# Loading part of w2's last row into five slots of 24 other partitions, in a one-core adaLN decode block

## The chip, the cores and the metric

The kernel runs on one core of one Trainium2 chip. The metric is device time in microseconds (us) of that core. Three runs of the kernel before gave 235.51, 235.61 and 235.60 us, median 235.6.

## What is computed

One decode step of a transformer block for a batch of two tokens, all in float32: a modulation by `c`, attention over the last 4096 places of a key/value cache, and a feed-forward part with SiLU.

```python
mod = (_silu(c) @ w_mod).reshape(c.shape[0], 6, 1, -1)
sa, ca, ga, sb, cb, gb = (mod[:, 0], mod[:, 1], mod[:, 2], mod[:, 3], mod[:, 4], mod[:, 5])
h = _layernorm(x, axis=-1) * (1 + ca) + sa
x = x + ga * _A_ref(h, A_k_cache, A_v_cache, A_wq, A_wo)   # 32 heads of 128, 8 of keys/values
h = _layernorm(x, axis=-1) * (1 + cb) + sb
x = x + gb * _B_ref(h, B_w1, B_w2)                         # silu(h @ w1) @ w2
return x
```

The batch is 2, the width D is 512 and the hidden width F is 1792. The weights and the used part of the cache come to 97.5 MB, each byte of which is read from memory once.

## The kernel before

**Order of the loads.** One engine's queue, SP, issues every large load, in program order: `w_mod`, `wq`, then eight pairs of cache pieces (4 MB each), `wo` in two loads, `w1` in two (L511 to L514: 2688 KB, then 896 KB), and `w2` in four (L599 to L604: 2048, 768, 512 and 256 KB). They land in a ring of eight slots of 16 KB in each of the 128 partitions, so a load waits until what stood in its slot has been used. The hardware counts landings in semaphores. The framework that builds the program gives each load from SP or ACT one of eight such semaphores (DMAHW0 to DMAHW7), in the order of the issues, and makes a load wait until the load that used the same semaphore before it, eight issues earlier, has landed.

**The feed-forward part.** Row `f` of `w2` with `f = 14 p + t` lies in partition `p` as tile `t` of 14, each of 512 columns. The hidden vector is `uT` (L659), laid out in the same way with 32 columns for each `t`, of which columns 0 and 16 hold the two tokens. TensorE takes `uT[:, t]` as weights and `w2`'s tile `t` as moving data:

- tiles 0 to 7 with 512 columns at a time into the bank `acc_yw`, each tile in one of four groups of 32 output partitions (L661 to L669)
- tiles 8 to 10 into `acc_y`, where each of the four groups takes 128 of the 512 columns (L671 to L679)
- `gather` (L548) copies `acc_yw` to SBUF, one half on ACT and the other on VectorE, and adds its four groups up into `acc_y` with four matmuls
- tiles 11 to 13 into two banks `acc_l` of 64 columns for each group (L684 to L694). Tile 13 is the last load

VectorE then multiplies by `gb`, adds the residual (L696 to L704), and SP stores 4 KB (L706). `busy` (L564) runs matmuls whose result is thrown away.

**What sets the order.** All of this is written with `inorder` (L312), which keeps the written order on its engine, so on TensorE everything from `acc_yw` on stands as the program has it. SP, TensorE and VectorE each do their own list in order, and a wait at the head of a list holds all that stands behind it.

Of the kernel before, what the change touches and what calls it, by code (L numbers as in the profile page):

```python
# [10 lines left out]
ALU = mybir.AluOpType  # L11
AX = mybir.AxisListType

P = 128
B, D = 2, 512
HQ, HKV, DH = 32, 8, 128
G = HQ // HKV
F = 1792
EPS = 1e-5
RING = 8  # L20


@with_exitstack
def adaln_block(
# [19 lines left out]
    nc = tc.nc  # L44
# [16 lines left out]
    def const(shape, name):  # L61
        return consts.tile(shape, F32, name=name)

    def bank(tag, name):
        return (psum1 if tag in "CO" else psum).tile([P, 512], F32, tag=tag, name=name)


    slots, turn_of = ring.tile([P, RING, 4096], F32, name="slots"), [0]

    def stream(n=1):  # L70
        i = turn_of[0]
        if n % 2 == 0:
# [15 lines left out]
    def load_runs(w, per, lo, hi):  # L88

        e = w.shape[1]  # L90
        n = -(-(hi - lo) * e // 4096)
        t = stream(n)[:, : (hi - lo) * e].rearrange("p (q e) -> p q e", e=e)
        nc.sync.dma_start(t, w.rearrange("(p q) e -> p q e", q=per)[:, lo:hi, :])
        return t
# [5 lines left out]
    ident = const([P, P], "ident")  # L100
# [6 lines left out]
    for b in range(B):  # L107
# [53 lines left out]
    odd = const([P, 2], "odd")  # L161
    nc.vector.tensor_reduce(
        odd, ident.rearrange("p (a r) -> p r a", r=2), axis=AX.X, op=ALU.add
    )

    selg0, selg = const([P, G], "selg0"), const([P, B, G], "selg")
# [42 lines left out]
    qbd = [const([P, 4, B, 4, 32], f"qbd{n}") for n in range(2)]  # L209
# [11 lines left out]
    def silu_exp(t, name, shape):  # L221

        e = once.tile(shape, F32, tag="silu", name=name)
        nc.vector.tensor_scalar(e, t, -1.0, 87.0, op0=ALU.mult, op1=ALU.min)
        nc.scalar.activation(e, e, AF.Exp)
        nc.vector.tensor_scalar(e, e, 1.0, None, op0=ALU.add)
        nc.vector.reciprocal(e, e)
        return e
# [64 lines left out]
    hT, uT = const([P, 4, 32], "hT_b"), const([P, F // P, 32], "uT")  # L293
# [6 lines left out]
    for n in range(2):  # L300
        for k in range(4):
            wv = wqt[:, k, :].rearrange("p (n s g m) -> p n g s m", n=2, s=4, g=G)
            for g in range(G):
# [4 lines left out]
                    start=(k == 0),  # L308
                    stop=(k == 3),
                )  # L310

    inorder = tc.keep_in_program_order  # L312
# [199 lines left out]
    for lo, hi in ((0, 3), (3, 4)):  # L512
        wt = load_runs(w1, 4, lo, hi)
        w1t.extend(wt[:, k, :] for k in range(hi - lo))  # L514

    rx = once.tile([P, B, HKV // 2, 2, G], F32, tag="rx", name="rx")
    for b in range(B):
        nc.vector.tensor_mul(
# [5 lines left out]
    for r in (0, 64):  # L524
# [4 lines left out]
            start=True,  # L529
            stop=True,  # L530
# [33 lines left out]
    def busy(n):  # L564

        for _ in range(n):
            inorder(nc.tensor.matmul(  # L567
                junk[0:32, :],
                id4,
                quad.rearrange("p m y -> p (m y)"),  # L570
                start=True,
                stop=True,
            ))
# [5 lines left out]
    for q in range(28):  # L579
        g = q % 4  # L580
# [4 lines left out]
            start=(q < 4),  # L585
            stop=(q >= 24),
        ))
    for q in range(28, 32):
        for g in range(4):
# [4 lines left out]
                start=(q == 28),  # L594
                stop=False,
            ))
    gather(ao, acc, "acc_o_sb", False, True)
    busy(1)
    T2, WIDE = F // P, 8  # L599
    w2t = {}  # L600
    for lo, hi in ((0, WIDE), (WIDE, 11), (11, 13), (13, T2)):
        wt = load_runs(w2, T2, lo, hi)
        for tt in range(lo, hi):
            w2t[tt] = wt[:, tt - lo, :]  # L604
    aoT = once.tile([P, 4, 32], F32, tag="zp", name="aoT")
    nc.vector.transpose(aoT, ao.rearrange("p (m k) -> p k m", k=4))
    x1T = once.tile([P, 4, B], F32, tag="x1T", name="x1T")
# [19 lines left out]
    for k in range(4):  # L627
        for g in range(4):
# [4 lines left out]
                start=(k == 0),  # L633
                stop=(k == 3),
# [22 lines left out]
        )  # L657
    sg = silu_exp(z, "sgh", [P, T2, B])
    nc.vector.tensor_mul(uT[:, :, 0:32:16], z, sg)  # L659
    yw = bank("D", "acc_yw")  # L660
    for tt in range(WIDE):  # L661
        g = tt % 4
        inorder(nc.tensor.matmul(  # L663
            yw[32 * g : 32 * g + 32, :],
            uT[:, tt, :],
            w2t[tt],
            start=(tt < 4),
            stop=(tt >= WIDE - 4),
        ))  # L669
    y = bank("D", "acc_y")[:, :P]  # L670
    for tt in range(WIDE, 11):  # L671
        for g in range(4):
# [4 lines left out]
                start=(tt == WIDE),  # L677
                stop=False,
# [2 lines left out]

    H = P // 2
    yl = [bank("A", f"acc_l{h}")[:, :H] for h in range(2)]
    for tt in range(11, T2):  # L684
        for h in range(2):
            for g in range(4):
                lo = g * P + h * H
                inorder(nc.tensor.matmul(
                    yl[h][32 * g : 32 * g + 32, :],
                    uT[:, tt, :],  # L690
                    w2t[tt][:, lo : lo + H],
                    start=(tt == 11),
                    stop=(tt == T2 - 1),
                ))  # L694
    yp = once.tile([P, P], F32, tag="xp", name="yp")
    inorder(nc.vector.tensor_mul(yp, y, gb))  # L696
    inorder(nc.vector.tensor_add(yp, yp, x1))
# [1 line left out]
    for h in range(2):  # L699
        r = slice(h * H, (h + 1) * H)  # L700
        inorder(nc.vector.tensor_mul(yo[:, r], yl[h], gb[:, r]))
    for h in range(2):
        r = slice(h * H, (h + 1) * H)
# [30 lines left out]
```

## Time and profile before

| what | us |
|---|---|
| time, median of three runs | 235.6 |
| profiled execution, first to last instruction (its span) | 233.7 |
| median of the runs less that span | 1.9 |
| TensorE busy | 160.2 |
| VectorE busy | 115.6 |
| ScalarE busy | 28.5 |
| chain that ended last: share that is a transfer | 60% |

Of the profiled execution only the span is recorded, no time of its own beside it. The span is the time of one execution under the profiler, so times in the trace are compared with each other, and the 1.9 us is what the runs add around it.

To read it: a transfer is moved by 16 DMA engines at once. A row of the timeline gives the start and the length of a group of instructions that follow each other on one engine; SPq is SP's own list, in which an entry's length is the time of the issue, not of the transfer. The list of DMA issues gives the time from an issue to the landing of the whole load, where something waited for it. TensorE does a float32 matmul in two passes, so it shows twice as many records as the program has matmuls.

### The profile page before, as it was taken

The page shows a single profiled execution, that of the slowest core. Times are in us where ns is not written, and L with a number is a line of the kernel's source. Part 1 is how long each engine was busy: PE and PEld are TensorE (multiplying, and loading weights), DVE is VectorE, ACT ScalarE, POOL GpSimd, SP SyncE. Part 2 cuts the span into 40 slices and gives each one's busy share as a digit, 9 for nine tenths or more (in the row PEclk, how much of TensorE's full clock was granted, in tenths as well). Part 3 has the DMA queues.
Part 4 walks back from the last instruction along what each step waited for, and adds up shares of the span by engine and source line. Part 5 has one row for each costly group of instructions (what it writes and reads, how often), then busy time and mean ns, then how long its engine had stood idle before and what let it go on. Part 6 is the DMA issues. An engine that isn't in the chain of part 4 may idle for free.

```text
span 233.7 us, 2571 instructions
## 1 busy us (share of the span) xinstructions
PE 160.2 (69%) x1070; PEld 43.1 (18%) x1070; DVE 115.6 (49%) x179; ACT 28.5 (12%) x64; POOL 10.6 (5%) x35
## 2 busy tenths in 40 slices
PE   0005916959577839787689759758769777869784
PEld 0001401211111111221111202201112122314223
DVE  3004140178795758696197189249559540101232
ACT  1100210000311120120210201111030031002020
POOL 8600010000000000000000000000000000000000
PEclk9999975879979997999979988999997999999999
DMA  7998998999999999999999999999999999989991
GB/s 269 446 520 381 426 471 359 440 443 428 415 421 449 440 443 421 421 423 449 443 437 426 415 429 449 437 437 429 404 444 443 437 423 471 446 362 427 423 412 57
DMA packets 3795, 97.68 MB, mean 418 GB/s; under 512 B 433, under 2 KB 457, under 8 KB 969
## 3 DMA queue, kind: packets, MB, share of 16 engines
q1 hardware_dynamic: 3768, 97.53, 97.2%
q8 instruction: 8, 0.13, 0.2%
q14 instruction: 3, 0.02, 0.0%
q10 hardware_dynamic: 16, 0.00, 0.0%
HBM read 97.53 MB, written 0.00 MB: 417 GB/s over the span
## 4 chain that ended last, share of the span: by engine, by line
DMA 60%; issue 17%; DVE 14%; PE 6%; POOL 1%; POOLq 0%; SPq 0%; ACT 0%; DVEq 0%
DMA slots<-in_A_k_cache_dram 22%; DMA slots<-in_A_wq_dram 14%; DMA slots<-in_B_w_dram 12%; DMA slots<-in_A_v_cache_dram 12%; DVE kT L363 11%; PE q L304 3%; PE o L450 2%; DVE zp L422 1%; PE acc_yw L663 1%; DVE xp L420 1%; PE acc_y L673 0%; DVE xc L102 0%; POOL qg L321 0%; DVE qT L317 0%; PE acc_y L554 0%
## 5 line engine op out<-in xcount | busy, mean ns | idle before, releaser
L363 DVE STREAM_TRANSPOSE kT<-slots 128x1024 f32<-128x1024 f32 x64 | 73.7, 1210 | 22.9 <-DMA slots<-in_A_k_cache_dram 22.8
L376 PE MATMUL s<-kT,qbd 128*32 128x512 f32 x256 | 68.5, 703 | 17.9 <-DVE kT L363 17.0
L450 PE MATMUL o<-slots,ptb 128*32 128x512 f32 x256 | 29.1, 595 | 2.2 <-DMA slots<-in_A_v_cache_dram 2.2
L376 PEld LDWEIGHTS s<-kT,qbd 128*32 128x32 f32 x256 | 9.8, 113 | 66.9 <-DVE kT L363 62.9
L271 PE MATMUL m_a<-slots,scT 128*32 128x256 f32 x32 | 4.4, 507 | 20.4 <-DVE scT L263 20.4
L304 PE MATMUL q<-slots,hq_T 128*32 128x512 f32 x64 | 9.7, 773 | 7.4 <-DMA slots<-in_A_wq_dram 7.4
L450 PEld LDWEIGHTS o<-slots,ptb 128*32 128x32 f32 x256 | 7.7, 109 | 16.7 <-issue 16.6
L406 ACT COPY bias<-bp 128x1 f32<-128x1 f32 x8 | 1.3, 159 | 75.8 <-PE bp L404 75.8
L386 DVE TENSOR_REDUCE mx<-s 128x1 f32<-128x512 f32 x8 | 5.5, 691 | 9.6 <-PE s L376 9.6
L567 PE MATMUL junk<-quad,id 128*32 128x512 f32 x22 | 10.2, 596 | 0.0
L437 ACT ACTIVATE ptb<-pT,odd 128x256 f32<-128x256 f32 x16 | 6.7, 472 | 26.0 <-PE pT L429 26.0
L422 DVE TENSOR_TENSOR zp<-xp,quarter 128x1024 f32<-128x1024 f32 x8 | 9.8, 1225 | 0.2
L429 PE MATMUL pT<-zp,mix 128*32 128x256 f32 x64 | 5.8, 438 | 4.0 <-DVE zp L422 4.0
L317 DVE STREAM_TRANSPOSE qT<-q 128x512 f32<-128x512 f32 x2 | 1.4, 717 | 13.5 <-PE q L304 12.0
L581 PE MATMUL acc_o<-slots,oTn 128*32 128x512 f32 x56 | 6.2, 593 | 2.3 <-DMA slots<-in_A_wo_dram 2.3
L460 ACT COPY ob<-o 128x512 f32<-128x512 f32 x8 | 4.7, 586 | 24.4 <-PE o L450 24.4
L552 DVE COPY acc_o_sb<-acc_o 128x256 f32<-128x256 f32 x1 | 0.4, 425 | 14.1 <-ACT acc_o_sb L551 14.1
L388 PE MATMUL mT<-ident,mx 128*1 128x128 f32 x16 | 3.0, 270 | 6.3 <-DVE mx L386 6.3
L420 DVE STREAM_TRANSPOSE xp<-pr 128x512 f32<-128x512 f32 x8 | 5.5, 685 | 3.4 <-ACT pr L408 3.4
L257 DVE STREAM_TRANSPOSE cT<-xc 128x128 f32<-128x128 f32 x1 | 0.4, 401 | 13.7 <-DMA xc<-in_c_dram 13.7
L274 PE MATMUL m_sp<-slots,scT 128*32 128x512 f32 x32 | 7.2, 730 | 0.0
L468 PE MATMUL o_all<-ob,selh 128*64 128x128 f32 x64 | 5.9, 313 | 0.8 <-ACT ob L460 0.8
(140 smaller groups left out, 93.7 us busy)
## 6 DMA issues: line engine op xcount, KB each, us to landing
slots<-in_A_k_cache_dram SPq DMA_DIRECT2D x8, 4096.0 KB, 27.6
slots<-in_A_v_cache_dram SPq DMA_DIRECT2D x8, 4096.0 KB, 27.7
slots<-in_w_mod_dram SPq DMA_DIRECT2D x1, 6144.0 KB, 17.2
slots<-in_A_wo_dram SPq DMA_DIRECT2D x1, 6144.0 KB
slots<-in_B_w_dram SPq DMA_DIRECT2D x1, 2688.0 KB
slots<-in_A_wo_dram SPq DMA_DIRECT2D x1, 2048.0 KB, 29.5
slots<-in_B_w_dram SPq DMA_DIRECT2D x1, 2048.0 KB
slots<-in_B_w_dram SPq DMA_DIRECT2D x1, 896.0 KB
```

The lines of the kernel that those rows point to most:

```text
L274: nc.tensor.matmul(m_sp[r, :], scT[:, k, :], cd[:, g], start=(k == 0), stop=(k == 3))
L304: nc.tensor.matmul(q_ps[n][32 * g : 32 * g + 32, :], hq_T[:, k, :], wv[:, n, g], start=(k == 0), stop=(k == 3),)
L363: inorder(nc.vector.transpose(kT[s, j][:, 32 * c : 32 * c + 32, :], kt[s].rearrange("p (n j r) -> p j n r", j=4, r=32)[:, j, 32 * c : 32 * ...
L376: inorder(nc.tensor.matmul(s_ps[s][r : r + 32, :], qbd[h // 4][:, h % 4, b, j, :], kT[s, j][:, 32 * c : 32 * c + 32, e:32:2], start=(j == ...
L420: inorder(nc.vector.transpose(xp, pr[s]))
L422: inorder(nc.vector.tensor_mul(zp, xp[:, None, :, 0:16].to_broadcast([P, 4, 16, 16]), quarter[:, :, None, None].to_broadcast([P, 4, 16, 16 ...
L429: inorder(nc.tensor.matmul(tp[32 * i : 32 * i + 32, :], mix.rearrange("p v e -> p (v e)"), zp.rearrange("p y t x -> p (y t) x")[:, :, 4 * ...
L437: inorder(nc.scalar.activation(ptb[s % 2][:, :, e, :], tp.rearrange("p (w z) -> p w z", z=16), AF.Copy, scale=odd[:, e : e + 1],))
L450: inorder(nc.tensor.matmul(o_ps[s][r : r + 32, :], ptb[s % 2][:, w].rearrange("p e z -> p (e z)"), vt[s].rearrange("p (c w m f d) -> p c f ...
L468: inorder(nc.tensor.matmul(o_all[r : r + 64, :], selh[:, m, lo : lo + 2 * HQ], o_sb[s][:, m * DH : (m + 1) * DH], start=(s == 0 and m < 2) ...
L567: inorder(nc.tensor.matmul(junk[0:32, :], id4, quad.rearrange("p m y -> p (m y)"), start=True, stop=True,))
L581: inorder(nc.tensor.matmul(acc[32 * g : 32 * g + 32, :], oTn[:, q, :], wot[q], start=(q < 4), stop=(q >= 24),))
```

## The change

In the last of the 14 tiles of `w2`, columns 384 to 511 (the last group of 128) of partitions 8 to 127 no longer come with the last load. Those 120 pieces of 512 bytes go to 24 other partitions (0 to 11 and 32 to 43), five to a partition, in eight loads of 3 by 5 pieces that stand in the program right behind `w1`'s second load. The place they go to is `qbd[0]`, which held queries for the first half of the heads and is free by then. The last load becomes two: 8 partitions of 128 columns, and 128 partitions of 384 columns.

So that the matmuls find the hidden values in the same partitions, a product with a 0/1 matrix `away` moves them: `uj` is `uT`'s last tile spread over five slots by `slot`, `up` is the product on TensorE, and VectorE copies it into `uF`. The last group's 128 columns are then made by five matmuls of 48 partitions and one of 8 in each half, in place of one of 128.

```diff
+NE, NR, NJ = 3, 4, 5
...
+    own = P - 2 * NR * NJ * NE
+    away, slot = const([P, 48], "away"), const([P, NJ], "slot")
+    nc.gpsimd.memset(away, 0.0)
+    for h in range(2):
+        nc.vector.tensor_reduce(
+            away[:, 32 * h : 32 * h + NE * NR].rearrange("p (e r) -> p e r", e=NE),
...
+        )
+    nc.vector.tensor_reduce(
+        slot,
...
+    )
...
+    T2, WIDE = F // P, 8
+    w2p = w2.rearrange("(p t) e -> p t e", t=T2)
+    spare = qbd[0].rearrange("p s b j c -> p (s b j c)")
+    far = spare[:, : NJ * P].rearrange("p (j m) -> p j m", j=NJ)
+    uF = spare[:, NJ * P : NJ * (P + 32)].rearrange("p (j n) -> p j n", j=NJ)
+    uj = spare[:, NJ * (P + 32) : NJ * (P + 32 + B)].rearrange("p (j b) -> p j b", j=NJ)
+    nc.gpsimd.memset(uF, 0.0)
+    for h in range(2):
+        for r in range(NR):
+            lo = own + 60 * h + NJ * NE * r
+            nc.sync.dma_start(
+                far[32 * h : 32 * h + NE * NR].rearrange("(e r) j m -> e r j m", r=NR)[:, r],
+                w2p[lo : lo + NJ * NE, T2 - 1, D - P :].rearrange("(j e) m -> e j m", e=NE),
+            )
...
-    T2, WIDE = F // P, 8
     w2t = {}
-    for lo, hi in ((0, WIDE), (WIDE, 11), (11, 13), (13, T2)):
+    for lo, hi in ((0, WIDE), (WIDE, 11), (11, 13)):
         wt = load_runs(w2, T2, lo, hi)
         for tt in range(lo, hi):
             w2t[tt] = wt[:, tt - lo, :]
+    w2l = stream(1)[:, :D]
+    nc.sync.dma_start(w2l[0:own, D - P :], w2p[0:own, T2 - 1, D - P :])
+    nc.sync.dma_start(w2l[:, : D - P], w2p[:, T2 - 1, : D - P])
...
     nc.vector.tensor_mul(uT[:, :, 0:32:16], z, sg)
+    nc.vector.tensor_mul(
+        uj,
+        uT[:, T2 - 1, 0:32:16][:, None, :].to_broadcast([P, NJ, B]),
+        slot[:, :, None].to_broadcast([P, NJ, B]),
+    )
...
+    up = bank("C", "up")[:48, : NJ * B]
+    inorder(nc.tensor.matmul(
+        up, away, uj.rearrange("p j b -> p (j b)"), start=True, stop=True
+    ))
+    nc.vector.tensor_copy(uF[:48, :, 0:32:16], up.rearrange("p (j b) -> p j b", b=B))
     y = bank("D", "acc_y")[:, :P]
...
-    for tt in range(11, T2):
+    def last(h, g, lhs, rhs, start=False, stop=False):
+        inorder(nc.tensor.matmul(
+            yl[h][32 * g : 32 * g + 32, :], lhs, rhs, start=start, stop=stop
+        ))
+
+    for tt in range(11, T2 - 1):
         for h in range(2):
             for g in range(4):
                 lo = g * P + h * H
...
+                last(h, g, uT[:, tt, :], w2t[tt][:, lo : lo + H], start=(tt == 11))
+    for h in range(2):
+        for j in range(NJ):
+            last(h, 3, uF[:48, j, :], far[:48, j, h * H : h * H + H])
+        last(
+            h, 3, uT[0:own, T2 - 1, :], w2l[0:own, 3 * P + h * H : 3 * P + h * H + H], stop=True
+        )
+    for h in range(2):
+        for g in range(3):
+            lo = g * P + h * H
+            last(h, g, uT[:, T2 - 1, :], w2l[:, lo : lo + H], stop=True)
```

On SP, the loads from `w1` on stood like this before (`slots` is the ring, `in_B_w` stands for `w1` and `w2`, 128x5376 is 128 partitions of 5376 numbers, and what is waited for stands in brackets):

```order
L93 DMA slots<-in_B_w_dram 128x5376 [waits DMAHW5_49,PE_49]
L93 DMA slots<-in_B_w_dram 128x1792 [waits DMAHW6_49,PE_49]
L93 DMA slots<-in_B_w_dram 128x4096 [waits PE_49]
L93 DMA slots<-in_B_w_dram 128x1536 [waits DMAHW7_49,PE_49]
L93 DMA slots<-in_B_w_dram 128x1024 [waits PE_49]
L93 DMA slots<-in_B_w_dram 128x512 [waits PE_49]
L706 DMA out_dram<-yo 4x2x128 [waits DVE_49]
```

and stand like this now, from `wo`'s two loads on:

```order
L94 DMA slots<-in_A_wo_dram 128x12288 [waits DMAHW3_49,DMAHW4_49,DVE_49,PE_49]
L94 DMA slots<-in_A_wo_dram 128x4096 [waits DVE_49]
L94 DMA slots<-in_B_w_dram 128x5376 [waits DMAHW5_49,PE_49]
L94 DMA slots<-in_B_w_dram 128x1792 [waits DMAHW6_49,PE_49]
L546 DMA qbd_157<-in_B_w_dram 3x5x128 [waits Pool_49]
L546 DMA qbd_157<-in_B_w_dram 3x5x128 x3
L546 DMA qbd_157<-in_B_w_dram 3x5x128 [waits DMAHW7_49,Activation_49]
L546 DMA qbd_157<-in_B_w_dram 3x5x128 [waits DMAHW0_49]
L546 DMA qbd_157<-in_B_w_dram 3x5x128 [waits DMAHW1_49]
L546 DMA qbd_157<-in_B_w_dram 3x5x128 [waits DMAHW2_49]
L94 DMA slots<-in_B_w_dram 128x4096 [waits DMAHW3_49,PE_49]
L94 DMA slots<-in_B_w_dram 128x1536 [waits DMAHW4_49,PE_49]
```

Eight issues have moved in between `w1`'s last load and `w2`'s first, and the last four of them, and every load behind them, wait on one of the eight landing semaphores.

On TensorE, the end of the program stood like this before (`acc_l_1106` and `acc_l_1107` are the two halves of 64 columns):

```order
L663 MATMUL acc_yw<-slots,uT 32x512 x8
L673 MATMUL acc_y<-slots,uT 32x128 x12
L554 MATMUL acc_y<-acc_y_sb,id_58 32x128 x4
L688 MATMUL acc_l_1106<-slots,uT 32x64 x4
L688 MATMUL acc_l_1107<-slots,uT 32x64 x4
```

with the last two rows twice more behind it, for tiles 12 and 13. Now it has `up` in front of tiles 8 to 10:

```order
L705 MATMUL acc_yw<-slots,uT 32x512 x8
L713 MATMUL up<-qbd_157,away 48x10
L720 MATMUL acc_y<-slots,uT 32x128 x12
L589 MATMUL acc_y<-acc_y_sb,id_58 32x128 x4
L732 MATMUL acc_l_1126<-slots,uT 32x64 x4
L732 MATMUL acc_l_1127<-slots,uT 32x64 x4
```

and, after the last two rows have come once more for tile 12, tile 13 at the very end as these six rows:

```order
L732 MATMUL acc_l_1126<-qbd_157 32x64 x5
L732 MATMUL acc_l_1126<-slots,uT 32x64
L732 MATMUL acc_l_1127<-qbd_157 32x64 x5
L732 MATMUL acc_l_1127<-slots,uT 32x64
L732 MATMUL acc_l_1126<-slots,uT 32x64 x3
L732 MATMUL acc_l_1127<-slots,uT 32x64 x3
```

In place of the last eight matmuls stand twelve into one group of 32 output partitions (the last of the four), and behind them six into the other three.

More of the change, by code (lines that the diff above doesn't have):

```diff
@@ L163, in adaln_block @@
         odd, ident.rearrange("p (a r) -> p r a", r=2), axis=AX.X, op=ALU.add
+    )
[5 more added lines that the diff above has]
+            away[:, 32 * h : 32 * h + NE * NR].rearrange("p (e r) -> p e r", e=NE),
+            ident[:, own + 60 * h : own + 60 * h + 60].rearrange(
+                "p (r j e) -> p e r j", r=NR, j=NJ
+            ),
+            axis=AX.X,
+            op=ALU.add,
+        )
+    nc.vector.tensor_reduce(
+        slot,
+        ident[:, own:].rearrange("p (hr j e) -> p j hr e", j=NJ, e=NE),
+        axis=AX.XY,
+        op=ALU.add,
     )
@@ L687, in adaln_block @@
                 lo = g * P + h * H
[L688 to L694, printed above, removed]
+                last(h, g, uT[:, tt, :], w2t[tt][:, lo : lo + H], start=(tt == 11))
[9 more added lines that the diff above has]
+            last(h, g, uT[:, T2 - 1, :], w2l[:, lo : lo + H], stop=True)
     yp = once.tile([P, P], F32, tag="xp", name="yp")
```

## Prediction

> **What bounds the kernel now.** I read the page first, then the chain that ended last, then single stretches of the end.
>
> ```profile
> span 233.7 us, 2571 instructions
> DMA  7998998999999999999999999999999999989991
> q1 hardware_dynamic: 3768, 97.53, 97.2%
> 197.41 28.93 DMA slots<-in_B_w_dram
> 226.47 1.92 PE acc_yw L663 x16
> ```
>
> The second line cuts the span into 40 slices: the DMA engines are full from the second to the last but one, and the third says that this is SP's queue, at 97% of all 16 engines. The kernel is as long as its stream of loads plus what follows the last bytes. The fourth and fifth lines are from the chain: `w2`'s first load (2048 KB) is issued at 197.41, lands at 226.34, and TensorE starts on it at 226.47. So a microsecond in which no load is in the queue is a microsecond of time, and so is one added behind the stream.
>
> ```profile
> 221.40:226.30 4.90, 4.25 (x23) 1.06 (x22) 2.10 (x8) 1.77 (x3) 0.00 (x0) 1.00 0.98 416
> 219.30:221.40 2.10, 1.97 (x21) 0.81 (x21) 0.00 (x0) 0.00 (x0) 0.00 (x0) 1.00 1.03 440
> L93 SPq DMA_DIRECT2D slots<-in_B_w_dram x6: 328/328/328, 190.2 to 212.7; - x6
> slots<-in_B_w_dram SPq DMA_DIRECT2D x1, 256.0 KB, 17.3
> ```
>
> In a table by stretches the last number is GB/s: 416 to 440, I take 430. 2048 KB are 2.10 MB, or 4.88 us (4.77 to 5.04). The trace states no landing for `w1`'s second load, but it is next in the queue ahead of those bytes: 226.34 - 4.88 = **221.46**. The last load (issued at 212.7, 17.3 to landing) lands at 230.0.
>
> **Part one: the eight loads on SP.** Each load takes the next of eight landing semaphores and waits until the load eight issues earlier has landed. Counted in the order of the change: the fifth small load waits for `wo`'s first load, the sixth for `wo`'s second, the seventh for `w1`'s first, the eighth for `w1`'s second. Queued behind the eighth on SP are all of `w2`'s loads.
>
> Before, `w2`'s first load was issued 24 us ahead of the moment when its bytes moved. Now it can't be issued before `w1`'s last byte has landed, at 221.46, and at that moment nothing but a few 512-byte pieces is in the queue. The stream runs dry.
>
> ```profile
> slots<-in_w_mod_dram SPq DMA_DIRECT2D x1, 6144.0 KB, 17.2
> ...
> 0.74 0.39 SPq L93 DMA_DIRECT2D slots<-in_w_mod_dram  x1
> 2.57 0.73 SPq L113 DMA_DIRECT2D xc<-in_A_x_dram  x1
> 231.11 0.63 SPq L706 DMA_DIRECT2D out_dram<-yo  x1
> 1.20:1.70 0.50, 0.00 (x0) 0.00 (x0) 0.00 (x0) 0.00 (x0) 0.42 (x2) 1.00 0.00 0
> 1.70:2.20 0.50, 0.00 (x0) 0.00 (x0) 0.41 (x1) 0.00 (x0) 0.50 (x4) 1.00 4.15 1278
> 231.80:232.35 0.55, 0.00 (x0) 0.00 (x0) 0.00 (x0) 0.00 (x0) 0.00 (x0) 1.00 0.00 0
> 232.35:232.50 0.15, 0.00 (x0) 0.00 (x0) 0.00 (x0) 0.00 (x0) 0.00 (x0) 1.00 0.11 27
> 229.80:230.00 0.20, 0.20 (x29) 0.20 (x20) 0.15 (x1) 0.00 (x0) 0.00 (x0) 1.00 0.00 0
> ```
>
> What filling it again costs is shown twice, at the first load and at the store, each into an empty queue. The store's issue ends at 231.11 + 0.63 = 231.74 and its first bytes move just after 232.35, `w_mod`'s ends at 1.13 and its first bytes move after 1.70: 0.6 us from the end of an issue to the first byte. In 1.70 to 2.20, 1278 GB/s x 0.5 us = 639 KB were started, 13 rows of 48 KB, so 13 of 16 engines began within 0.5 us and three later. No piece starts in 229.80 to 230.00, yet the load lands at 230.0: 0.3 us from the last piece to the landing.
>
> The sum, step by step: `w1` landed 221.46; SP wakes 0.04 (VectorE's last row below ends at 231.09, the store's issue begins at 231.11); the eighth small load's issue 0.63 (between a plain 0.33 and `x`'s 0.73, nearest to the store's); 0.05 to the next, my guess; `w2`'s issue 0.33; to the first byte 0.6; spread of the engines' starts 0.4 (0.1 to 0.9); 4.88 for the bytes; 0.3 to the landing. That is 228.7 in place of 226.34: **+2.35 us** (+1.6 to +3.0).
>
> The rest of SP's part is covered. The first four small loads go out at about 196 to 199, behind `w1`'s in the queue. The later `w2` loads wait on small loads that have landed by then. The last two loads carry 61 KB less than the 256 KB before, 0.14 us, but it will be seen that the last landing is no longer what ends last.
>
> The Trainium skill, "DMA: Bandwidth & Descriptors", in the section on why a DMA increments its semaphore by 16, says that a load is spread over the largest number up to 16 that divides both slowest dimensions, so over 3 engines here. No row of this page separates the engines. In the forecast it costs nothing, as the small loads land in the dry stretch; where they didn't, three of 16 engines would be later, a rival below.
>
> **Part two: TensorE behind the last loads.**
>
> ```profile
> 226.47 1.92 PE L663 MATMUL acc_yw<-slots,uT 128*32 128x512 f32 x16 [0.82 <-DMA slots<-in_B_w_dram]
> 228.32 0.86 PE L673 MATMUL acc_y<-slots,uT 128*32 128x128 f32 x24
> 229.54 0.97 PE L688 MATMUL acc_l<-slots,uT 128*32 128x64 f32 x47
> 199.57 1.08 PE L541 MATMUL oq<-on,quad 128*128 128x64 f32 x8 [0.81 <-DVE on L538]
> 221.07 0.38 PE L638 MATMUL var_b<-vs,mean 128*128 128x2 f32 x2
> 228.91 0.42 DVE L552 COPY acc_y_sb<-acc_yw 128x256 f32<-128x256 f32 x1 [3.39 <-ACT acc_y_sb L551]
> 230.46 0.35 DVE L701 TENSOR_TENSOR yo<-acc_l,mod_sp 128x64 f32<-128x64 f32 x2
> 230.74 0.35 DVE L704 TENSOR_TENSOR yo<-yo,yp 128x64 f32<-128x64 f32 x2
> ```
>
> Four groups of output partitions run side by side, so passes count in rounds of four. The first row is 4 rounds of 512 columns, the second 6 of 128: 1280 columns make 1.06 us, 0.83 ns a column, with 0.22 us to drain. A round of 64 columns is 0.053 us. Tile 13 was 16 passes in 4 rounds, 0.21 us. Now twelve matmuls, 24 passes, all go into the **same** group, one after the other: 24 x 0.053 = 1.27 us, and the other six, 12 passes in 4 rounds, take 0.21 behind them. That the pieces are 48 partitions high doesn't shorten a pass, whose time follows its columns. Bounds: if four passes could run side by side, 0.32; if each had to wait for its weights as in `oq`, (1.08 - 0.22) / 8 = 0.107 a pass, 2.6. The first row's rate is the nearest, since its weights too are 32 columns wide: 1.27.
>
> Was TensorE waiting there, so that this hides? Tiles 11 and 12 were 8 rounds from 229.54, until 229.96, and the last load came at 230.03. There are 0.07 us of cover, and `up` uses it. `up` fills all rows of the array, as `var_b` does: 0.03 to 0.4 us on TensorE ahead of `acc_y`. Of that, the half of `gather` that waited for VectorE's copy (ends 229.33) hides most: `acc_y`'s rounds ended at 228.96, now up to 0.3 later. With `uF`'s copy ahead of that copy on VectorE, I take 0.1 us. So tile 13 begins 0.1 us later relative to the landings and takes 1.27 more: **+1.37 us** (+0.4 to +2.7). VectorE's tail (230.46 to 231.09) moves along unchanged. Now TensorE, not the last load, ends last.
>
> The rest is hidden: three reductions on VectorE and one memset on POOL in the first 3 us lie under `w_mod`'s transfer (issued at 0.74, landed 17.2 later), and `uj` under the wait for `w2`. If that cover were gone, each would cost some 0.2 us.
>
> **The sum.** Span 233.7 + 2.35 + 1.37 = 237.4, and the runs add 1.9: the median is 235.6, so **239.3 us**.
>
> **Rivals.**
>
> 1. The clock of TensorE falls.
>
> ```profile
> 224.63 1.02 PE L567 MATMUL junk<-quad,id 128*32 128x512 f32 x2
> 117.44 2.20 PE L376 MATMUL s<-kT,qbd 128*32 128x512 f32 x6 [2.83 <-DVE kT L363]
> 117.77:121.18 3.41, 3.39 (x16) 0.42 (x12) 3.38 (x4) 0.00 (x0) 0.00 (x0) 0.50 0.96 413
> 156.16 2.22 PE L376 MATMUL s<-kT,qbd 128*32 128x512 f32 x8 [2.85 <-DVE kT L363]
> 155.31:158.73 3.42, 2.19 (x8) 0.29 (x8) 3.39 (x4) 0.00 (x0) 0.00 (x0) 1.00 0.95 412
> ```
>
> After `busy` TensorE is idle from 225.65 to 226.47 now, and would be to 228.85, 3.2 us. After 2.83 us idle the granted clock was 0.50 for the next 3.4 us; after 2.85 it stayed at 1.00. If it halves from about 230.4 on, the rounds that then run at half speed (`acc_y` 0.64, the two halves of `gather` 0.43, tiles 11 and 12 0.42) take 1.5 us more, which gives **240.8**. By the Trainium skill, "TensorE: Matmul & The Clock Gate", section "Part 1: The HAM clock gate", the rate halves after an idle window of about 3.4 us; by that alone 3.2 us would not halve it, but the row after 2.83 us shows less to be enough.
>
> 2. The waits on SP cost nothing, because the stream has something else to move. Then the small loads are in its way: by the page's rule three engines carry their 61 KB, at 3/16 of 430 GB/s 0.76 us. With TensorE's 1.37: **237.7**. Against it: the order shows the wait, and the trace has no other load to move.
>
> 3. The passes into one group overlap in part, 0.32 in place of 1.27: **238.3**. Against it: the rate above is the same in both rows with four groups busy, which leaves none idle.
>
> 4. Not slower: the loads are issued early, the last load is 61 KB shorter, and TensorE has the pieces done while it waits. Then 0.14 us goes: **235.5**. It decides from the point where the added rounds are shorter than TensorE's idle time ahead of the last landing; that is 0.07 us, against 1.27.
>
> **Chances.** Forecast 0.50, rival 1 0.27, rival 2 0.08, rival 3 0.10, rival 4 0.05. A measurement of this kernel tells about 0.2% (0.5 us) from no change. Rival 4 is divided between faster (0.02) and the same (0.03); all others are slower, 0.95. The range reaches from 238.0, below rival 3, to 241.0, above rival 1; the bounds of the two terms inside the forecast fill the space between, and rivals 2 and 4 stay out.
>
> **What would show it.** In the changed kernel's trace: SP's list with `w2`'s first issue at about 222, in place of 197.4, and a wait of SP on `w1`'s load; a stretch of about 1 us after 221.5 in which almost nothing moves; `acc_yw` starting at about 228.8; the last 36 passes of `acc_l` taking some 1.5 us beyond the last landing; SP's store at about 234.8. The forecast is wrong if `w2`'s bytes flow without a gap after `w1`'s, or if the matmuls into one group take far less than 0.05 us a pass.

## The result and the profile after

The changed kernel takes **243.35 us** (five runs, 242.42 to 243.98) where the kernel before takes 235.6 us: ratio 1.0326, 95% interval 1.0308 to 1.0344. It is slower by 7.75 us. The forecast was +3.7 us and its range ended at 241.0, so the direction was right and the size was not.

The page of the kernel after, first the span, then the DMA engines in 40 slices (busy tenths, and GB/s), then SP's queue:

```profile
span 241.3 us, 2642 instructions
...
DMA  7998989999999999999999999999999999996850
GB/s 269 506 444 348 522 348 432 435 436 429 435 435 435 432 435 435 435 432 435 435 435 435 432 435 435 435 435 432 431 429 429 426 473 407 394 424 224 362 216 1
...
q1 hardware_dynamic: 3928, 97.53, 94.4%
```

The same 97.53 MB are moved, and up to the 36th slice there is no hole. The 37th slice (217 to 223 us) has 224 GB/s in place of some 430. The last slice of 6 us has 1 GB/s, where before the last slice still had 57. TensorE is at work there, and the loads are over. So there are two losses to look for, one in the stream and one behind it.

SP's own list, start and length of the issues:

```profile
196.68 25.25 SPq L546 DMA_DIRECT2D qbd<-in_B_w_dram  x8
222.03 1.30 SPq L94 DMA_DIRECT2D slots<-in_B_w_dram  x3
...
238.55 0.63 SPq L762 DMA_DIRECT2D out_dram<-yo  x1
```

The eight small loads (L546) hold SP for 25 us. `w2`'s first three loads are issued at 222.03, where the first stood at 197.41 before. The chain of waits says what held them:

```profile
196.30 24.91 DMA slots<-in_B_w_dram
221.23 0.71 SPq L546
...
222.03 7.32 DMA slots<-in_B_w_dram
229.35 0.14 issue
```

The chain goes through `w1`'s second load, then the eighth small load, issued when that has landed at 221.2, then `w2`'s first load, which lands at 229.35, then TensorE. What the DMA engines and the clock did meanwhile is in a table by stretches of 1 us (behind the stretch and its length: busy time of TensorE, its weight loads, VectorE, ScalarE and GpSimd; then TensorE's granted clock, the DMA share and GB/s):

```profile
220.00:221.00 1.00, 1.00 (x14) 0.27 (x6) 0.00 (x0) 0.00 (x0) 0.00 (x0) 1.00 0.41 157
221.00:222.00 1.00, 1.00 (x14) 0.49 (x18) 0.17 (x1) 0.71 (x2) 0.00 (x0) 1.00 0.00 0
222.00:223.00 1.00, 1.00 (x13) 0.30 (x6) 0.05 (x1) 0.84 (x1) 0.00 (x0) 1.00 0.02 8
223.00:224.00 1.00, 1.00 (x4) 0.23 (x3) 0.96 (x3) 0.00 (x0) 0.00 (x0) 1.00 1.19 262
224.00:225.00 1.00, 1.00 (x4) 0.21 (x2) 0.64 (x4) 0.23 (x1) 0.00 (x0) 1.00 0.82 328
...
228.00:229.00 1.00, 0.00 (x0) 0.00 (x0) 0.00 (x0) 0.00 (x0) 0.00 (x0) 0.76 0.90 379
229.00:230.00 1.00, 0.51 (x4) 0.23 (x8) 0.00 (x0) 0.00 (x0) 0.00 (x0) 0.50 0.98 412
...
235.00:236.00 1.00, 1.00 (x45) 0.89 (x37) 0.58 (x2) 0.00 (x0) 0.00 (x0) 0.83 0.00 0
```

From 221 to 223 almost nothing moves (the 8 GB/s are the eighth small load), and from 223 to 225 the rate is 262 and 328 GB/s, in place of 430. In the clock's column, TensorE falls to half speed: 0.76 in 228 to 229 and 0.83 in 235 to 236 place the change at 228.5 and back at 235.3, 6.8 us at 0.50. TensorE's list shows what fell into that:

```profile
229.49 3.64 PE L705 MATMUL acc_yw<-slots,uT 128*32 128x512 f32 x16 [4.05 <-DMA slots<-in_B_w_dram]
...
235.03 0.77 PE L732 MATMUL acc_l<-slots,uT 128*32 128x64 f32 x32
235.74 0.74 PE L732 MATMUL acc_l<-qbd 48*32 48x64 f32 x10
236.41 0.29 PE L732 MATMUL acc_l<-slots,uT 8*32 8x64 f32 x2
236.63 0.74 PE L732 MATMUL acc_l<-qbd 48*32 48x64 f32 x10
237.31 0.65 PE L732 MATMUL acc_l<-slots,uT 8*32 8x64 f32 x14
```

TensorE was idle for 4.05 us ahead of `acc_yw` (0.82 before), and `acc_yw` takes 3.64 us in place of 1.92. The last row joins two passes of 8 partitions with the twelve of 128. With these rows and those of before, the way to the store's issue (231.11 before, 238.55 now) divides into three stretches:

| stretch | before | after | more | forecast |
|---|---|---|---|---|
| landing of `w2`'s first load | 226.34 | 229.35 | +3.01 | +2.35 |
| from there to the first pass of `acc_l` (229.53, 235.03) | 3.19 | 5.68 | +2.49 | +0.1 |
| from there to the store's issue | 1.58 | 3.52 | +1.94 | +1.27 |
| sum | | | +7.44 | +3.72 |

Theory: the first stretch is the dry stream, the second is the half clock, and the third is tile 13's passes into one group with something that the forecast left out. Rivals: the small loads themselves are expensive to move; the clock is not what matters; the third stretch is a wait for loads (against this speaks the last row of the table by stretches: no DMA engine moves anything there, and TensorE is busy throughout).

### The profile page after: what moved, and what is told of

Read it like the earlier page. It is cut to its first block, busy times and chain, and to the rows that moved or that the text cites. A ratio compares the mean times of both kernels' runs of the same rounds, so it can differ in the third digit from the quotient of the medians.

```text
span 241.3 us, 2642 instructions
## 1 busy us (share of the span) xinstructions
PE 165.4 (69%) x1092; PEld 45.2 (19%) x1092; DVE 116.4 (48%) x184; ACT 28.5 (12%) x64; POOL 10.8 (4%) x37
## 3 DMA queue, kind: packets, MB, share of 16 engines
q1 hardware_dynamic: 3928, 97.53, 94.4%
HBM read 97.53 MB, written 0.00 MB: 404 GB/s over the span
## 4 chain that ended last, share of the span: by engine, by line
DMA 73%; DVE 15%; PE 9%; issue 1%; POOL 1%; SPq 0%; ACT 0%; DVEq 0%; POOLq 0%
DMA slots<-in_A_k_cache_dram 34%; DMA slots<-in_A_wq_dram 14%; DMA slots<-in_B_w_dram 13%; DMA slots<-in_A_v_cache_dram 11%; DVE kT L383 11%; PE q L324 4%; DVE zp L442 2%; PE acc_yw L705 2%; PE o L470 1%; PE acc_l L732 1%; DVE xp L440 1%; PE acc_y L720 1%; DVE xc L103 0%; DVE qT L337 0%; SPq L546 0%
## 5 line engine op out<-in xcount | busy, mean ns | idle before, releaser
L396 PE MATMUL s<-kT,qbd 128*32 128x512 f32 x256 | 70.5, 704 | 18.6 <-DVE kT L383 17.6
L470 PE MATMUL o<-slots,ptb 128*32 128x512 f32 x256 | 30.8, 624 | 2.1 <-DMA slots<-in_A_v_cache_dram 2.1
L324 PE MATMUL q<-slots,hq_T 128*32 128x512 f32 x64 | 8.8, 708 | 8.2 <-DMA slots<-in_A_wq_dram 8.2
L294 PE MATMUL m_sp<-slots,scT 128*32 128x512 f32 x32 | 6.6, 711 | 0.0
L705 PE MATMUL acc_yw<-slots,uT 128*32 128x512 f32 x16 | 3.6, 1059 | 4.1 <-DMA slots<-in_B_w_dram 4.1
```

The costliest lines, as they stand in the source:

```text
L294: nc.tensor.matmul(m_sp[r, :], scT[:, k, :], cd[:, g], start=(k == 0), stop=(k == 3))
L324: nc.tensor.matmul(q_ps[n][32 * g : 32 * g + 32, :], hq_T[:, k, :], wv[:, n, g], start=(k == 0), stop=(k == 3),)
L396: inorder(nc.tensor.matmul(s_ps[s][r : r + 32, :], qbd[h // 4][:, h % 4, b, j, :], kT[s, j][:, 32 * c : 32 * c + 32, e:32:2], start=(j == ...
L470: inorder(nc.tensor.matmul(o_ps[s][r : r + 32, :], ptb[s % 2][:, w].rearrange("p e z -> p (e z)"), vt[s].rearrange("p (c w m f d) -> p c f ...
L705: inorder(nc.tensor.matmul(yw[32 * g : 32 * g + 32, :], uT[:, tt, :], w2t[tt], start=(tt < 4), stop=(tt >= WIDE - 4),))
```

## The experiments

The expectations were written ahead of each run. Each run is compared with runs of the kernel before on the same chip (medians 235.49 to 235.56 us).

**The small loads where nothing waits for them.** The eight loads are issued one by one, seven behind the last pieces of the cache and one behind `wo`'s first load, so that none of their landings holds `w2`'s loads back. Everything else is as in the changed kernel.

```diff
         if s < STEPS:
             kt[s] = load_pair(k_cache, s)
+            if s > 4:
+                one()
         if s > 0:
             vt[s - 1] = load_pair(v_cache, s - 1)
+            if s > 4:
+                one()
...
         wt = load_runs(wo, 32, lo, hi)
+        one()
```

> The eight small loads go out one by one behind the last cache loads and wo's first load, so that eight issues back lies four big loads back and no wait for a landing holds w2's loads; the rest is as in the change. Theory A (the semaphore wait empties the stream, TensorE then idles and its clock halves, and the passes into one group come on top): w2's first load is issued at about 197 again, acc_yw starts by 227.4, the clock stays at 1.00 at the end, and only TensorE's added work for tile 13 and up remains: 237.5 us (236.9 to 238.6, the upper end if three DMA engines carry the pieces and land last). Rival B (the pieces of 512 bytes are slow in themselves wherever they stand): at least 241 us.

Measured: 237.96 us, ratio 1.0103 (1.0088 to 1.0118), as the theory had it. SP's and TensorE's lists:

```profile
197.47 13.82 SPq L94 DMA_DIRECT2D slots<-in_B_w_dram  x4
...
232.93 0.62 SPq L773 DMA_DIRECT2D out_dram<-yo  x1
```

```profile
226.41 1.92 PE L716 MATMUL acc_yw<-slots,uT 128*32 128x512 f32 x16 [0.84 <-DMA slots<-in_B_w_dram]
...
229.44 0.25 PE L743 MATMUL acc_l<-slots,uT 128*32 128x64 f32 x2
...
230.12 0.74 PE L743 MATMUL acc_l<-qbd 48*32 48x64 f32 x10
230.79 0.29 PE L743 MATMUL acc_l<-slots,uT 8*32 8x64 f32 x2
231.01 0.74 PE L743 MATMUL acc_l<-qbd 48*32 48x64 f32 x10
231.69 0.65 PE L743 MATMUL acc_l<-slots,uT 8*32 8x64 f32 x14
```

`w2`'s first issue is back at 197.47 and `acc_yw` starts at 226.41, 0.06 us before the old time. So the loads' bytes cost nothing that can be seen; the place of their issues cost 5.4 of the 7.75 us. From `acc_yw`'s start to the first pass of `acc_l` it is 3.03 us (3.06 before), so `up` is hidden wholly, and the second stretch of the table was not its doing. From there to the store it is 3.49 us, +1.91 over before: the third stretch stays as it was.

**The small loads alone.** The kernel before with the eight loads added in the changed kernel's place; nothing reads them.

```diff
+    for h in range(2):
+        for r in range(NR):
+            lo = own + 60 * h + NJ * NE * r
+            nc.sync.dma_start(
+                far[32 * h : 32 * h + NE * NR].rearrange("(e r) j m -> e r j m", r=NR)[:, r],
+                w2p[lo : lo + NJ * NE, T2 - 1, D - P :].rearrange("(j e) m -> e j m", e=NE),
+            )
     rx = once.tile([P, B, HKV // 2, 2, G], F32, tag="rx", name="rx")
```

> The eight small loads stand where the change has them, but nobody reads them: the last load is whole, and tile 13 is eight matmuls as before; up and the copies are gone. Theory A: the stream runs dry and the clock halves as in the change, without the 1.8 us of tile 13 and the 0.3 us of up: 241.0 us (240.3 to 241.7), acc_yw at about 229.5 at a clock of 0.50. Rival D (TensorE's added work is what makes up most of the loss): under 239 us.

Measured: 240.68 us, ratio 1.022 (1.0203 to 1.0237), within the theory's range, but with other parts than it had: the landing came later and the half clock was shorter. Its rows stand beside those of the next.

**The wait alone.** The kernel before, without small loads; GpSimd copies one number of `w1`'s last tile into the place of `w2`'s first load, so that this load waits for `w1`'s landing. (The first lines of the cut keep `w2`'s loads in program order.)

```diff
+        d = nc.sync.dma_start(t, w.rearrange("(p q) e -> p q e", q=per)[:, lo:hi, :])
+        if per == F // P:
+            tc.keep_in_program_order(d)
...
     for lo, hi in ((0, WIDE), (WIDE, 11), (11, 13), (13, T2)):
+        if lo == 0:
+            ahead = slots[:, turn_of[0] % RING, :]
+            nc.gpsimd.tensor_copy(ahead[0:1, 0:1], w1t[3][0:1, 0:1])
         wt = load_runs(w2, T2, lo, hi)
```

> The kernel before, in which w2's first load waits for w1's last landing by a copy of one number on POOL into its slot; no small load, no change on TensorE. Theory A: the same dry stretch, a little shorter since a copy stands in place of a small load's issue: w2's first issue at about 221.7, acc_yw at about 229.0, and 240.5 us if the clock halves as in the change, 238.3 us if it doesn't. Rival B (it is the small pieces): 235.6 to 236.2 us.

Measured: 240.48 us, ratio 1.0212 (1.019 to 1.0233), the number given for a halved clock. The chain of this kernel, and its lists of TensorE and SP:

```profile
221.96 7.51 DMA slots<-in_B_w_dram
```

```profile
229.61 3.64 PE L668 MATMUL acc_yw<-slots,uT 128*32 128x512 f32 x16 [3.81 <-DMA slots<-in_B_w_dram]
```

```profile
236.53 0.63 SPq L711 DMA_DIRECT2D out_dram<-yo  x1
```

Not one small load is needed for the loss: a wait of `w2`'s first issue for `w1`'s landing gives +4.9 us. It has the two parts of the theory. The landing, at 229.47, is late by 229.47 - 226.34 = 3.13 us, and `acc_yw` runs at half speed: from its start to the store it is 6.92 us, where before it was 4.64, +2.28 us.

The kernel with the small loads alone says the same with another division:

```profile
229.99 3.03 PE L676 MATMUL acc_yw<-slots,uT 128*32 128x512 f32 x16 [4.29 <-DMA slots<-in_B_w_dram]
```

Here the clock was halved for one stretch of 3.4 us only, from 230.7 to 234.1, and from `acc_yw` to the store, issued at 235.75, it is 5.76 us, +1.12: half as long at half speed, half the loss. Its landing, at 229.86, is late by 3.52 us.

**The clock.** The changed kernel with more thrown-away matmuls ahead of `w2`, so that TensorE is idle for less.

```diff
-    busy(3)
+    busy(7)
```

> The change with seven in place of three matmuls of thrown-away work in front of acc_yw, 3.4 us more, so that TensorE idles 0.6 us in place of 4.1 before w2's first load. Theory A: landings as in the change, clock 1.00 to the end, acc_yw 1.9 us in place of 3.6, in all 2.5 us less: 240.9 us (240.4 to 241.5). Rival C (TensorE is slow there for another reason than its idle time): 243.3 us, acc_yw still 3.6.

Measured: 241.2 us, ratio 1.0242 (1.0227 to 1.0258), again as expected. TensorE's list and SP's:

```profile
223.50 6.17 PE L602 MATMUL junk<-quad,id 128*32 128x512 f32 x14
230.26 1.92 PE L705 MATMUL acc_yw<-slots,uT 128*32 128x512 f32 x16 [0.60 <-DMA slots<-in_B_w_dram]
```

```profile
236.79 0.61 SPq L762 DMA_DIRECT2D out_dram<-yo  x1
```

The granted clock is 1.00 to the end and `acc_yw` takes 1.92 us again. From its start to the store it is 6.53 us, against 9.06 in the changed kernel: the half clock cost **2.53 us**. (In the medians it is 2.15 us; in this profile `w2`'s first load landed 0.8 us later than in the profile of the changed kernel, since `w1` did.) What is left, 6.53 - 4.64 = 1.89 us, is the price of tile 13. The first experiment gives it from other rows, 232.93 - 226.41 - 4.64 = 1.88, and the wait alone gives the clock as 2.28 on less work. So the 7.44 us are 3.01 of late landing, 2.53 of clock and 1.9 of tile 13.

That the longer idle time brought the half clock is shown by this run. When exactly the clock changes was not tested, but the records of the granted clock show a pattern. In all twelve profiles every stretch at half or at full clock lasts a whole multiple of 3.41 us (but for the last, which the end of the record cuts). Between such points, the kernel before, the changed kernel and the one with the small loads alone read (the number behind the comma is TensorE's busy time, the third from the end its clock):

```profile
114.35:117.77 3.42, 0.59 (x6) 0.14 (x4) 1.63 (x2) 0.59 (x1) 0.00 (x0) 1.00 1.02 441
151.90:155.31 3.41, 1.42 (x16) 0.21 (x8) 0.45 (x1) 0.59 (x1) 0.00 (x0) 1.00 1.03 442
```

```profile
225.10:228.51 3.41, 0.34 (x1) 0.00 (x0) 0.38 (x2) 0.00 (x0) 0.00 (x0) 1.00 0.98 420
228.51:231.93 3.42, 2.44 (x12) 0.69 (x16) 0.00 (x0) 0.00 (x0) 0.00 (x0) 0.50 0.96 395
231.93:235.34 3.41, 3.41 (x54) 2.09 (x50) 0.58 (x3) 0.37 (x1) 0.00 (x0) 0.50 0.15 53
```

```profile
227.26:230.68 3.42, 0.69 (x8) 0.34 (x12) 0.00 (x0) 0.00 (x0) 0.00 (x0) 1.00 0.95 401
230.68:234.09 3.41, 3.41 (x39) 1.91 (x35) 0.42 (x1) 0.37 (x1) 0.00 (x0) 0.50 0.62 247
```

A stretch with 0.59 us of work was followed by half clock, one with 1.42 us was not: these are the prediction's idle times of 2.83 and 2.85 us, of which the second lay across two stretches. At half clock, 2.44 us of work in a stretch did not bring the full clock back, and 3.41 us did. Counted over the twelve profiles up to 228 us, a stretch at full clock with less than 1.4 us of work was always followed by half clock and one with more than 2.1 us never; at half clock, less than 2.6 us never brought the full clock back and more than 2.85 us always did; between these bounds both occur. So the records speak for the work in a fixed stretch as what decides, and not for the length of the idle time. The points lie elsewhere in each execution, and with them the cost: 2.53 us here, 1.12 with the small loads alone.

**Passes into one group.** The kernel before with all its loads; `up`, with what feeds it and its copy, and twenty passes of 48 partitions over zeros are added ahead of tile 13. In one kernel they all go into the last group, in the other into the four groups in turn.

```diff
+    for h in range(2):
+        for j in range(NJ):
+            last(h, 3, uF[:48, j, :], far[:48, j, h * H : h * H + H])
```

and in the second `(5 * h + j) % 4` in place of 3.

> No small load and the last load whole, as before; up stays, and ten of the twelve new matmuls of tile 13 run on a slot of zeros, all into the last group, ahead of tile 13's eight old ones. So only TensorE's added work is there. Theory A (passes into one group follow each other, 20 x 0.056, and a change of the matmuls' height costs about 0.11 each, twice, and up 0.1): 1.4 us more, 237.0 us (236.6 to 237.3). Rival (there is slack ahead of the last landing that hides most of it): under 236.2 us.

> The same with the ten matmuls dealt out over the four groups in turn. Theory A: only the group matters, 20 passes are 5 to 7 rounds, 0.28 to 0.4 us, with two changes of height and up 0.6 to 0.8 us in all: 236.2 us (236.0 to 236.5). Rival (it is the number of passes, not their group, that costs): the same 237.0 us as with one group.

Measured: 237.11 us in one group, ratio 1.0071 (1.0057 to 1.0084); 236.25 us in four, ratio 1.0037 (1.0026 to 1.0048), both where the theory put them. The twenty passes and what follows, in one group:

```profile
229.93 1.30 PE L721 MATMUL acc_l<-qbd 48*32 48x64 f32 x20
231.16 0.43 PE L721 MATMUL acc_l<-slots,uT 128*32 128x64 f32 x16
```

and in four:

```profile
230.17 0.53 PE L721 MATMUL acc_l<-qbd 48*32 48x64 f32 x20
230.63 0.43 PE L721 MATMUL acc_l<-slots,uT 128*32 128x64 f32 x16
```

From start to start that is 1.23 us against 0.46. Passes into one group follow each other, and four groups run side by side, as the forecast had it.

**Changes of height.** The height of a matmul is the number of partitions that it reads. In the rows of the changed kernel and of the first experiment, ten passes of 48 partitions take 0.67 us from start to start, and twenty take 1.23 here. So a pass is (1.23 - 0.67) / 10 = 0.056 us, and 0.11 us are left over at each change to another height. Two passes of 8 partitions fit that: 231.01 - 230.79 = 0.22 = 2 x 0.056 + 0.11. The next kernel is the first experiment with the two matmuls of 8 partitions side by side, which saves two changes.

```diff
         for j in range(NJ):
             last(h, 3, uF[:48, j, :], far[:48, j, h * H : h * H + H])
+    for h in range(2):
         last(
```

> As e1_spread, with the two matmuls of 8 partitions next to each other behind the ten of 48, so that the height changes three times in place of five. Theory A (a change of height costs about 0.11 us beside the passes): 0.2 us less than e1_spread, 237.7 us, and the trace shows 20 passes of 48 partitions in a row at 0.056 us. Rival (each matmul of 8 partitions costs the 0.22 us itself): no change, 238.0 us.

Measured: 237.63 us, ratio 1.0096 (1.0082 to 1.0109), where the first experiment had 237.96 and 237.7 was expected. Its four runs spread from 237.43 to 238.27, so the median alone doesn't decide against the rival's 238.0; the rows do.

```profile
230.03 1.30 PE L743 MATMUL acc_l<-qbd 48*32 48x64 f32 x20
231.26 0.76 PE L743 MATMUL acc_l<-slots,uT 8*32 8x64 f32 x16
```

From the first pass of 48 partitions to the end it is 1.99 us, against 2.22: 0.23 for two changes. The trace's records of single passes show the same: the twenty passes follow each other at 0.056 us, and at the changes from 48 to 8 and from 8 to 128 partitions the next pass comes after 0.145 us and the one behind it after another 0.08, together 0.11 more than two usual steps.

**The pieces left out.** Neither the small loads nor the products with them; only the last load in two parts, with the last group's product over 8 partitions.

```diff
+    w2l = stream(1)[:, :D]
+    nc.sync.dma_start(w2l[0:own, D - P :], w2p[0:own, T2 - 1, D - P :])
+    nc.sync.dma_start(w2l[:, : D - P], w2p[:, T2 - 1, : D - P])
...
+    for h in range(2):
+        last(
+            h, 3, uT[0:own, T2 - 1, :], w2l[0:own, 3 * P + h * H : 3 * P + h * H + H], stop=True
+        )
```

> The 120 pieces of w2 (the last 128 columns of its last row in partitions 8 to 127) are left out altogether, loads and matmuls, and the last load is the two short ones of the change: all that the change could win, with none of its price. Theory: the last landing comes 0.15 us sooner at most, and VectorE's yp, which follows from acc_yw and not from the last load, ends at the same moment as before: 0 to 0.15 us less, 235.5 us. Rival (the last load alone sets the end, and two loads of fewer bytes take less by more than their bytes): 235.0 us or less.

Measured: 236.29 us, ratio 1.0034 (1.0021 to 1.0046). A miss: with the whole price left out the kernel is still 0.75 us slower than before.

```profile
226.67 1.92 PE L691 MATMUL acc_yw<-slots,uT 128*32 128x512 f32 x16 [0.29 <-DMA slots<-in_B_w_dram]
...
229.76 1.38 PE L713 MATMUL acc_l<-slots,uT 128*32 128x64 f32 x46
```

The start of `acc_yw` is 0.2 us later, and `acc_l`'s rows last 1.38 us, where before they lasted 0.97. Fewer partitions and the same number of passes, yet 0.4 us more. Two runs take that apart on the kernel before, with its loads untouched.

**The order alone, then the height alone.** First, tile 13's matmuls of the last group stand ahead of the others, with 128 partitions as before. Then the same with 8 partitions.

```diff
+    for h in range(2):
+        last(h, 3, T2 - 1, P)
+    for h in range(2):
+        for g in range(3):
+            last(h, g, T2 - 1)
```

with 8 in place of `P` in the second.

> The kernel before, with one thing changed: tile 13's two matmuls of the last group (128 partitions, as before) come first, then the six of the other groups. No load and no height of a matmul changes. If passes into one group follow each other at 0.055 us, four of them stand alone ahead of four rounds of three: tile 13 lasts 4 x 0.055 = 0.22 us longer, and nothing hides it: 235.75 us against 235.54 (235.65 to 235.85). If the 0.75 us of the run with the pieces left out came from its loads alone, this is 235.5.

> As the one above, but the last group's two matmuls read 8 partitions in place of 128 (120 rows of w2 are left out of the product; the loads are those of before). If each change of a matmul's height on TensorE costs 0.09 us by itself, two changes are added (128 to 8, 8 to 128), less what is hidden under the wait for the last load: 235.9 us (235.8 to 236.05). If the height costs nothing and the longer starts seen so far belong to the waits for loads, it is 235.75 like the one above; if 8 rows pass faster than 128, less.

Measured: the order alone 235.6 us, ratio 1.0007 (0.9998 to 1.0015), no difference clear of noise, where 235.75 was expected. With 8 partitions 235.97 us, ratio 1.0017 (1.0007 to 1.0026): near the number expected, but with twice the step to the kernel before it that two changes alone explain (0.37 us, not 0.18). The end of TensorE's list with the order alone:

```profile
229.73 0.25 PE L686 MATMUL acc_l<-slots,uT 128*32 128x64 f32 x2
...
229.79 0.95 PE L686 MATMUL acc_l<-slots,uT 128*32 128x64 f32 x46
```

and with 8 partitions:

```profile
229.67 0.22 PE L686 MATMUL acc_l<-slots,uT 128*32 128x64 f32 x1
...
229.67 1.41 PE L686 MATMUL acc_l<-slots,uT 128*32 128x64 f32 x47
```

From the first pass of `acc_l` to the end it is 1.01 us with the order alone (0.98 before) and 1.41 us with 8 partitions. The times alone would leave room for the 0.2 us expected of the order, since the interval reaches to 1.0015; in the rows it costs nothing that can be seen: the four passes of the last group run beside the other groups' passes that stand behind them, so the expectation that they would stand alone was wrong. At another height they do stand alone: 0.40 us more for two changes and four passes (2 x 0.11 + 4 x 0.056 = 0.44). In the second kernel only the height differs from the first, and no load does. So passes of these heights don't run side by side, and a change of height costs 0.11 us besides. Only 8, 48 and 128 partitions were run; which heights count as different is not shown. That accounts for 0.4 of the 0.75 us of the run with the pieces left out. The other 0.3 was not settled: 0.2 us of it is the later start of `acc_yw`, which falls between 226.22 and 226.69 in the profiles of the eight kernels whose stream doesn't run dry, the kernel before among them. But the five runs of the kernel with the pieces left out lie within 0.13 us of each other, so scatter from run to run is not the cause; it stays open.

## Why the prediction came out as it did

The direction was right, the size wrong. The sum "233.7 + 2.35 + 1.37" is 3.72 us short of the rows' 7.44 us more, by three terms: the stretch with the clock, for which it has no term (2.39), the landing of `w2`'s first load (0.66) and tile 13 (0.67). The first is the step that failed most: the forecast let TensorE keep its full clock through the longer wait, and the half clock cost 2.53 us.

**Part one, the mechanism: right.** The eighth small load waits for `w1`'s second load, everything of `w2` stands behind it, the stream runs dry, and the chain of waits names this step. `w2`'s first issue was forecast for 222.18 and came at 222.03; `w1` had landed 0.25 us earlier than forecast (221.21), and the small load's issue took 0.71 us in place of 0.63.

**Part one, the size of the refill: too small.** The step that failed is "to the first byte 0.6; spread of the engines' starts 0.4 (0.1 to 0.9)": from the start of the issue to the landing the sum gave 0.33 + 0.6 + 0.4 + 4.88 + 0.3 = 6.51 us. Measured were 7.32, and 7.51 in the kernel with the wait alone, which has no small loads. In the trace's records of single pieces, `w2`'s first piece begins at 223.01, 0.65 us after the end of its issue, as forecast, and fourteen of the sixteen engines begin by 223.46. But the first piece of each of these fourteen, 16 KB, took 1.08 to 1.60 us, where one in the full stream takes 0.61. The engine that ended last began at 223.15: 1.60 us and seven pieces of 0.61 bring it to 229.0, and the landing follows at 229.35. The forecast took the engines' starts from `w_mod`'s row and then counted full speed from the first byte on; in the same records of the kernel before, `w_mod`'s first pieces took 2.1 to 3.0 us and later ones 1.8. With +3.01 for +2.35 the landing was just beyond the bound given (+3.0).

**Rival 1, the clock: it came true, on top of the forecast, and was priced too low.** The forecast took an idle time of 3.2 us, between "halves" and "stays". The later landing (+0.66 us) and an earlier end of `busy` (225.44 in place of 225.65) made it 4.05. After 4.05, 3.81 and 4.29 us idle the clock was halved, and after 0.28 to 0.84 it never was. With these times only 0.34 of the 3.41 us up to 228.51 was work. The halving came at 228.5 and not from 230.4 on, so all of `acc_yw` fell into it, which the rival had left out: 2.53 us in place of 1.5. Where the points of change fall in an execution could not be foreseen, so a part of the size was chance. By the Trainium skill, "TensorE: Matmul & The Clock Gate", section "Part 1: The HAM clock gate", the rate halves after an idle window of about 3.4 us; the three idle times above are longer than that and agree with it, the 2.83 us in the prediction's rows is shorter and halved the clock too. By the page alone the true idle time would have made this rival the forecast.

**Part two, passes into one group: right, with one term missing.** A pass took 0.056 us (forecast 0.053), they stood one after the other, and `up` is hidden (forecast 0.1). What failed is the sentence "That the pieces are 48 partitions high doesn't shorten a pass, whose time follows its columns". It is true of a pass, but it took the height to be without any price. Tile 13 changes height five times (128 to 48, 8, 48, 8, 128): 24 x 0.056 + 5 x 0.11 = 1.89 us, measured +1.91 without the wait and +1.94 with it.

**Rivals 2 to 4: wrong in the kernel as it stands.** Rival 2 (no waits) is what the first experiment builds; it gave 237.96 where that rival said 237.7, but for another reason: three engines for the pieces cost nothing that can be seen, in place of 0.76 us, and the changes of height cost 0.55. Rival 3 falls with the one-group run. Rival 4 falls even with the pieces left out.

**The range.** It was put together from cases that exclude each other: the forecast's bounds, or rival 1. But a longer refill makes the idle time longer and with it the half clock likelier and dearer, so the cases add up in one direction. The forecast's sum with the upper bound of part one, rival 1's 1.5 us and 0.5 us more in part two would have reached 242, still short of 243.35.

**What the trace doesn't show.** The profiled runs of the changed kernel and of the first experiment are 2.15 and 2.3 us longer than their spans, where before it was 1.9. These 0.2 to 0.4 us lie outside all rows and were not followed.

No kernel of these was faster than the one before. The shorter last load was worth at most the forecast's 0.14 us, and the run with the pieces left out shows that even without their price nothing of it arrives.

## What to carry to other kernels

A small load takes a landing semaphore like a large one, so before putting many into a queue that streams, count which load eight issues back each of them waits for; spread among early loads they cost nothing here, and in a row they cost 5.4 us. When a stream runs dry, price the refill with its slow first pieces and then ask whether TensorE, waiting for it, loses its full clock, since the second loss follows from the first. Behind the last landing, every pass into a single group of output partitions counts in full, and so does every change of a matmul's height.

## What the runs showed of the hardware that was not expected

- TensorE did not run passes of 8, 48 and 128 partitions side by side, even into different groups, and a change between them added 0.11 us to the 0.056 us of a float32 pass of 64 columns, also where the program has no wait at the change (8 to 48). Order among passes of one height cost nothing that could be seen (1.01 us against 0.98).
- The granted clock changed only at points a multiple of 3.41 us apart. After an idle time of 3.81 or 4.05 us the half clock lasted 6.8 us, through more than 5 us of steady work; after 4.29 us it lasted 3.4 us. In the rows the difference is the first stretch at half clock: TensorE worked 2.44 us of it in the changed kernel, and all 3.41 us with the small loads alone. This is read from the records; no run was made to test it.
- A stream that restarts on empty queues needs about 0.8 us more than its start delay and its bytes at full rate account for (7.3 to 7.55 us from issue to landing for 2 MB in four kernels, against 6.5). In the changed kernel the first 16 KB of most engines took 1.08 to 1.60 us, in place of 0.61.
